# Attention decode with a gated FFN on one core: another wait of the last query, an output product on four quadrants, and a meeting of the engines under the store

## The chip, the cores and the metric

The kernel runs on one core of a Trainium2 chip. The core has five engines with their own instruction streams: TensorE (PE, matrix products; its weight loads are listed as PEld), VectorE (DVE), ScalarE (ACT), GpSimd (POOL) and SyncE (SP, which here issues the transfers). Sixteen DMA engines move data between the chip's main memory and the core's on-chip memory, whose 128 partitions the engines read in parallel. PE writes its sums to a second on-chip memory, PSUM. Engines wait for one another by semaphores.

The metric is the device time of one execution in microseconds, the median of several runs. A profile comes from one further execution.

## The reference

One token goes through a block of attention with a cached K and V, and a gated FFN. Both have a residual and a layer norm in front. All data is float32.

```python
B, Sq, D = 1, 1, 640
H, Sk, Dh = 32, 8192, 192          # 32 heads, 8192 cached positions
F = 1536

q = (x @ wq).reshape(B, Sq, H, Dh)
scores = einsum("bhqd,bhkd->bhqk", q, k_cache) * (Dh ** -0.5)
p = softmax(scores)
o = einsum("bhqk,bhkd->bhqd", p, v_cache)
A(x) = o.reshape(B, Sq, H * Dh) @ wo

gate = x @ W_gate ; up = x @ W_up
B(x) = (gate * (gate > 0) * up) @ W_down

h  = x + A(layernorm(x))
h2 = h + B(layernorm(h))           # the output, 640 numbers
```

K and V of one head take 6.3 MB each, so the execution reads 446 MB in all and computes little with each number.

## The kernel before, in words

Each head's data is packed on the host into two transfers. The first is K (tile `kt`, 12,288 columns on 128 partitions). The second is V together with the head's 192 rows of `wo` and the next head's columns of `wq` (tile `vt0` for heads 1, 3, 5 and so on, `vt1` for heads 2, 4, 6 and so on). There is one `kt` and there are two `vt`. SP issues all loads in one queue, in the order K, V, K, V. It waits for `sp` (the scores of the head before are done, so `kt` is free) ahead of a K, and for `wo` (the output product that reads the same `vt` is done) ahead of a V.

A loop over pairs of heads runs on PE, DVE and ACT. For head n:

- PE makes the scores: 24 products in groups of four quadrants, that is four products of 32 output rows each that use different quarters of the array and of PSUM's partitions (`scores`, tile `sp`).
- PE then finishes the head before: `output(n, vt)` sums the value products over partitions (`po`), DVE's `combine` divides by the softmax's sum and places the head's 192 numbers as two columns in `o` (128 and 64 of them), and PE multiplies them by the rows of `wo` and adds to `acc`, which stays in PSUM for the whole execution. The 64 numbers are first spread by ACT into `o2` (`second`), with zeros in the other half of the partitions, since the 64 rows of `wo` are packed as two halves of 320 columns. PE's last product signals `wo`.
- DVE takes the maximum of the scores on each partition, PE transposes it, DVE takes the maximum of all, ACT makes the exponentials `p` and their sums, PE adds those over partitions (`pl`).
- PE then makes the query of the next head from the `wq` columns in the same `vt` (`query`, five products into `pq`).
- DVE makes 12 value products, j = 0 to 11, each over 1024 columns of `vt` with `p`, with the sum of each partition in `op[:, j]`. Between j = 5 and j = 6 it reads the next query out of `pq` (`columns`), which ACT turns into the operands of the next scores (`masks`).

The last head differs. Its V carries no `wq` columns and comes in four parts (`v0`, semaphores `vb`, `vb1`, `vb2`, `vb3`, three value products each, the fourth with the `wo` rows). DVE waits for each part where it needs it. The loop still makes a next query after it, from old data in the tile, and nobody uses it. For the heads before, the semaphores `vb1` to `vb3` are raised at the start so far that their waits are met.

After the loop come the last output product, ACT's copy of `acc` to `h4` with its sum, the mean and a transpose on DVE, and the FFN. PE multiplies by W_up and W_gate (10 steps of four quadrants), DVE makes the gated product and a transpose, PE multiplies by W_down (12 steps j of four quadrants), DVE adds the residual, and SP stores 640 numbers. The FFN's weights come last in SP's queue: W_up and four fifths of W_gate into `vt0`, the rest of W_gate and W_down (in five transfers) into `kt`. They are issued once the output product of the last but one head is done.

`acc` holds one row of the output, copied over partitions: before, partitions 0 to 63 hold columns 0 to 319, and partitions 64 to 127 the others.

At the end of the program the engines meet at a barrier, POOL clears all semaphores, and they meet again.

Of the kernel before, what the change touches and what calls it, by code (L numbers as in the profile page):

```python
# [6 lines left out]
AF = mybir.ActivationFunctionType  # L7
# [3 lines left out]
P, Q, NQ = 128, 32, 4  # L11
H, S, DH, D, F = 32, 8192, 192, 640, 1536
# [8 lines left out]
D2 = DH - P  # L21
DG, FG, HN = D // NQ, F // NQ, D // 2
KW = S + S // 2
WO = D + HN
# [31 lines left out]
        self.eng.wait_ge(self.c.sem, self.c.n)  # L56


def mha_decode_reglu_kernel(nc, x, w0, kk, vv, v0, w_up, w_gate, w_down, out):
    names = ("w0", "xr", "k", "k2", "va", "vb", "vb1", "vb2", "vb3", "qd", "qs", "sp", "mp", "pt", "m1", "rs",  # L60
             "pl", "q", "op", "po", "o", "o2", "wo", "cst", "st", "ffn0", "ffn1", "ffn2", "ffn3", "ffn4",
             "ffn5", "ffn6", "ffn7", "h4", "hm", "hc", "hr", "pu", "us", "pg", "gu", "pd", "o4", "out")
    s = {n: nc.alloc_semaphore("e_" + n) for n in names}

    def sb(name, shape):
        return nc.alloc_sbuf_tensor(name, shape, F32).ap()

    def ps(name, shape):
        return nc.alloc_psum_tensor(name, shape, F32).ap()
# [4 lines left out]
    xrow = sb("xrow", [1, D])  # L74
    ones = sb("ones", [P, P])
# [5 lines left out]
    blk = sb("blk", [P, NG])  # L81
    blk2 = sb("blk2", [P, NJ - NG])
    half = sb("half", [P, 2])
    side = sb("side", [P, 2, D2])
    pick = sb("pick", [P, 3, 2, C])
    st = sb("st", [P, 16])
    xc = sb("xc", [P, DJ])
# [8 lines left out]
    p = sb("p", [P, SG])  # L96
# [1 line left out]
    rl = sb("rl", [P, 1])  # L98
    op = sb("op", [P, NJ])
    o = sb("o", [P, 2])  # L100
    o2 = sb("o2", [P, P])
    h4 = sb("h4", [P, DG])
    hs1 = sb("hs1", [P, 1])
    hT = sb("hT", [P, DJ, Q])
    hc = sb("hc", [P, DJ, Q])
    hsq = sb("hsq", [P, DJ])
    us = sb("us", [P, FG])
    gu = sb("gu", [P, FG])
    guT = sb("guT", [P, FJ, Q])
    o4 = sb("o4", [P, DG])  # L110
# [6 lines left out]
    acc = ps("acc", [P, QB])  # L117
# [20 lines left out]
    def sync_fn(sy):  # L138
        sy.dma_start(wq0, w0).then_inc(s["w0"], 16)  # L139
        sy.sem_inc(s["k2"], 16 * (H - 1))  # L140
        for n in ("vb1", "vb2", "vb3"):
            sy.sem_inc(s[n], 16 * (H // 2 - 1))
        for h in range(H):
            if h > 0:
                sy.wait_ge(s["sp"], h)
            if h < H - 1:
                sy.dma_start(kt, kk[h]).then_inc(s["k"], 16)
            else:
                sy.dma_start(kt[:, 0:KW // 2], kk[h][:, 0:KW // 2]).then_inc(s["k"], 16)
                sy.dma_start(kt[:, KW // 2:KW], kk[h][:, KW // 2:KW]).then_inc(s["k2"], 16)  # L150
            if h > 0:
                sy.wait_ge(s["wo"], h)
            if h < H - 1:
                sy.dma_start(vts[h % 2], vv[h]).then_inc(s["vb" if h % 2 else "va"], 16)
            else:
                W = JV * SG
                for i, n in enumerate(("vb", "vb1", "vb2", "vb3")):
                    c0, c1 = i * W, (i + 1) * W if i < 3 else KW + WO
                    sy.dma_start(vts[1][:, c0:c1], v0[:, c0:c1]).then_inc(s[n], 16)  # L159
        sy.wait_ge(s["wo"], H)  # L160
        for i, (dst, src, n) in enumerate(ffn):
            if i == 2:
                sy.wait_ge(s["sp"], H)
            sy.dma_start(dst, src).then_inc(s[n], 16)
        sy.wait_ge(s["o4"], 1)
        sy.dma_start(out[0].rearrange("o (g n) -> (o g) n", g=NQ), o4[0:P:Q, :]).then_inc(s["out"], 16)
        sy.wait_ge(s["out"], 16)

    def pool_fn(g):
        c = Chain(nc, g, "e_pool")  # L170
# [16 lines left out]
    def vector_fn(v):  # L187
        c = Chain(nc, v, "e_dve")
        ve, y, t = st[:, 0:1], st[:, 1:2], st[:, 2:3]
# [18 lines left out]
        c.sync()  # L208
        c(v.tensor_copy(same[:, 1:NG, :], same[:, 0:1, :].to_broadcast([P, NG - 1, C])))
        c(v.reduce_sum(blk2, low.rearrange("p (a c) -> p a c", c=C), axis=AX.X))  # L210
        c(v.tensor_copy(side, half[:, :, None].to_broadcast([P, 2, D2])))
        c(v.tensor_copy(pick[:, 2], half[:, :, None].to_broadcast([P, 2, C])))
        c.sync()
        v.sem_inc(s["op"], 1)
# [46 lines left out]
        with v.Fori(1, H + 1, 2) as i:  # L261
            i8 = i * 8 + 8
# [4 lines left out]
        hmean, hs2, hvar, hr = (st[:, i:i + 1] for i in range(9, 13))  # L267
# [20 lines left out]
    def scalar_fn(a):  # L288
        a.dma_start(xrow, x[0]).then_inc(s["xr"], 16)
        sd = st[:, 3:4]  # L290
        a.wait_ge(s["st"], 5)
        a.activation(sd, st[:, 7:8], AF.Sqrt, bias=eps).then_inc(s["st"])
        a.activation(st[0:1, 14:15], eps[0:1, :], AF.Exp)

        def masks(n):
            a.wait_ge(s["qd"], n)
            pk = pick.rearrange("p i a c -> p i (a c)")
            a.mul(qs[:, 0:2, :], pk[:, 0:2, :], q[:, 0:1])  # L298
            a.mul(qs[:, 2, :], pk[:, 2, :], q[:, 1:2]).then_inc(s["qs"])  # L299

        def second(n):
            a.wait_ge(s["o"], n)
            a.mul(o2, side.rearrange("p a c -> p (a c)"), o[:, 1:2]).then_inc(s["o2"])  # L303

        def head(n):
            second(n)
            a.wait_ge(s["m1"], n)
            a.activation(p, sp, AF.Exp, bias=m1, accum_out=rs).then_inc(s["rs"])  # L308
            masks(n + 1)

        masks(1)
        with a.Fori(1, H + 1, 2) as i:
            head(i)
            head(i + 1)
        second(H + 1)
        a.activation(st[0:1, 14:15], eps[0:1, :], AF.Sqrt)
        a.wait_ge(s["wo"], H + 1)
        for g in range(NQ):
            r = slice(g * Q, (g + 1) * Q)
            ins = a.activation(h4[r], acc[r, (g % 2) * DG:(g % 2 + 1) * DG], AF.Copy, accum_out=hs1[r])  # L320
        ins.then_inc(s["h4"])
        a.wait_ge(s["st"], 10)
        a.activation(sd, st[:, 11:12], AF.Sqrt, bias=eps).then_inc(s["st"])
        a.wait_ge(s["hr"], 1)
        a.wait_ge(s["pu"], 1)
        a.activation(us, sp[:, 0:FG], AF.Copy, scale=st[:, 12:13]).then_inc(s["us"])

    def tensor_fn(t):
        def mm(dst, lhsT, rhs, start, stop, **kw):
            return t.matmul(dst, lhsT, rhs, start=start, stop=stop, **kw)  # L330
# [7 lines left out]
        def scores():  # L338
            for u in range(NU):
                if u:  # L340
                    yield
                for k in range(3):
                    for g in range(NQ):
                        c0 = u * (KW // 2) + (k * NQ + g) * QB
                        ins = mm(sp[g * Q:(g + 1) * Q, u * QB:(u + 1) * QB], qs[:, k, :], kt[:, c0:c0 + QB],
                                 k == 0, k == 2)
            ins.then_inc(s["sp"])
            yield

        def output(n, vt):  # L350
            t.wait_ge(s["op"], n)
            mm(po[:, 0:NJ], same.rearrange("p a c -> p (a c)"), op, True, True).then_inc(s["po"])
            t.wait_ge(s["o"], n)
            for i in range(2):
                mm(acc[i * D2:(i + 1) * D2, 0:HN], o[:, 0:1].to_broadcast([P, D2]),
                   vt[:, KW + i * HN:KW + (i + 1) * HN], False, False, skip_group_check=True)
            t.wait_ge(s["o2"], n)
            mm(acc[:, 0:HN], o2, vt[:, KW + D:KW + WO], False, False, skip_group_check=True).then_inc(s["wo"])

        def head(i, b, i8):  # L360
            n = i + b if b else i
            t.wait_ge(s["qs"], n)
            sc = scores()
            k_wait(i, b, "k")
            next(sc)
            k_wait(i, b, "k2")
            next(sc)
            output(n, vts[1 - b])
            t.wait_ge(s["mp"], n)
            t.transpose(pt[:, 0:P], mp.to_broadcast([P, P]), ident).then_inc(s["pt"])  # L370
            t.wait_ge(s["rs"], n)
            mm(pl[:, 0:1], share, rs, True, True).then_inc(s["pl"])
            t.wait_ge(s["vb3" if b else "va"], i8)
            if b:
                t.wait_ge(s["vb"], i8)
            query(vts[b][:, KW + WO:VW])

        def k_wait(i, b, name):
            t.wait_ge(s[name], i * 16 + 16 * b if b else i * 16)
# [2 lines left out]
        t.wait_ge(s["st"], 1)  # L382
        mm(pt[:, 0:1], ones, st[:, 4:5], True, True).then_inc(s["st"])
        t.wait_ge(s["xr"], 16)
        for i in range(2):
            mm(acc[i * D2:(i + 1) * D2, 0:HN], ones[0:1, 0:D2], xrow[:, i * HN:(i + 1) * HN], True, False,
               skip_group_check=True)
        t.wait_ge(s["st"], 3)
        mm(pl[:, 0:1], ones, st[:, 6:7], True, True).then_inc(s["st"])
# [2 lines left out]
        with t.Fori(1, H + 1, 2) as i:  # L392
            i8 = i * 8 + 8
# [25 lines left out]
        for j in range(FJ):  # L419
            if j in cuts:  # L420
                t.wait_ge(s[f"ffn{3 + cuts.index(j)}"], 16)
            for g in range(NQ):
                ins = mm(pq[g * Q:(g + 1) * Q, 0:DG], guT[:, j, :], dn[:, j, g * DG:(g + 1) * DG],
                         j == 0, j == FJ - 1)
        ins.then_inc(s["pd"])

    with nc.Block() as block:
        block.sync(sync_fn)
        block.scalar(scalar_fn)
        block.gpsimd(pool_fn)  # L430
        block.vector(vector_fn)
        block.tensor(tensor_fn)
# [50 lines left out]
```

## Time and profile before

| | us |
|---|---|
| median of 3 runs | 1044.72 |
| lowest, highest | 1044.05, 1044.84 |
| the profiled execution's own time | 1045.74 |
| its span, from first to last instruction | 1043.8 |

| engine | busy us | share of the span |
|---|---|---|
| PE | 453.8 | 43% |
| PEld | 209.0 | 20% |
| DVE | 525.5 | 50% |
| ACT | 77.6 | 7% |
| POOL | 2.1 | 0% |

The profile lists, for each group of like instructions, the line, the engine, the operation, the tiles written and read, their shapes, the number of instructions, the busy time, the mean of one, and the idle time of the engine just before them with what ended it. The chain of waits starts at the last instruction and follows back what released each step. A window can be cut out of each view. PE's clock is not constant: the profile gives the share of full speed that was granted. On average it was 0.657 in this execution.

Nearly all of a float32 matmul's records come as two passes, so that three matmuls stand as x6.

### The profile page before, as it was taken

What the parts mean: (1) busy time and instruction counts of PE and PEld (TensorE: products, weight loads), DVE (VectorE), ACT (ScalarE), POOL (GpSimd) and SP (SyncE); (2) the same over time, 40 slices, a digit from 0 to 9 for tenths busy, and PEclk for the clock granted to TensorE, in tenths of its full rate; (3) what the DMA queues carried; (4) which work ended last, traced back from release to release, by engine and by line L of the source; (5) the groups of instructions that cost most, each with busy time, mean ns of one, the idle gap of its engine ahead of it and who ended that gap; (6) DMA issues with size and microseconds to landing.
All of it is one profiled execution on the core that took longest, in us unless ns stands there. A gap on an engine that the chain in (4) does not pass through costs nothing.

```text
span 1043.8 us, 6624 instructions
## 1 busy us (share of the span) xinstructions
PE 453.8 (43%) x2414; PEld 209.0 (20%) x2414; DVE 525.5 (50%) x1162; ACT 77.6 (7%) x179; POOL 2.1 (0%) x15
## 2 busy tenths in 40 slices
PE   4344353355353355343355343255343255343536
PEld 2122121122121122121122121122121122121213
DVE  1644465644465644465644465644465644465651
ACT  1000000000000000000000000000000000000001
POOL 0000000000000000000000000000000000000000
PEclk9667765666765666676666676766666766665667
DMA  9999999999999999999999999999999999999995
GB/s 397 445 423 429 433 448 422 444 423 431 431 448 422 444 423 429 431 448 424 444 421 431 431 446 424 441 426 431 431 443 426 441 426 431 431 443 426 421 429 247
DMA packets 11102, 445.97 MB, mean 427 GB/s; under 512 B 1237, under 2 KB 1241, under 8 KB 2010
## 3 DMA queue, kind: packets, MB, share of 16 engines
q1 hardware_dynamic: 11096, 445.92, 99.0%
q8 instruction: 2, 0.03, 0.0%
q10 hardware_dynamic: 2, 0.00, 0.0%
q14 instruction: 2, 0.02, 0.0%
HBM read 445.91 MB, written 0.00 MB: 427 GB/s over the span
## 4 chain that ended last, share of the span: by engine, by line
DMA 73%; PE 25%; DVE 1%; issue 0%; ACT 0%; SPq 0%; DVEq 0%
DMA kt<-in_kk_dram 70%; PE sp L330 23%; DMA vt<-in_v_dram 4%; PE pq L330 1%; DVE vt L135 1%; PE acc L330 0%; ACT h L320 0%; SPq L159 0%; DVE junk L135 0%; PE po L330 0%; DVE guT L284 0%; PE pt L330 0%; DVE gu L283 0%; PE pl L330 0%; SPq L139 0%
## 5 line engine op out<-in xcount | busy, mean ns | idle before, releaser
L135 DVE CUSTOM_DVE_ANT_0 vt<-vt,p 128x1024 f32<-128x1024 f32 x384 | 444.9, 1221 | 142.1 <-DMA vt<-in_vv_dram 142.1
L330 PE MATMUL sp<-kt,qs 128*32 128x512 f32 x1536 | 239.7, 789 | 342.1 <-DMA kt<-in_kk_dram 337.6
L330 PE MATMUL pq<-vt,xn 128*128 128x192 f32 x320 | 113.1, 539 | 159.0 <-DMA vt<-in_vv_dram 150.5
L330 PEld LDWEIGHTS sp<-kt,qs 128*32 128x32 f32 x1536 | 55.8, 140 | 512.6 <-DMA kt<-in_kk_dram 359.4
L135 DVE CUSTOM_DVE_ANT_0 junk<-blk,po,rl 128x8 f32<-128x8 f32 x66 | 12.0, 218 | 265.2 <-PE po L330 265.2
L330 PEld LDWEIGHTS pq<-vt,xn 128*128 128x128 f32 x320 | 97.9, 331 | 161.3 <-DMA vt<-in_vv_dram 78.8
L330 PE MATMUL acc<-vt,o 128*64 128x320 f32 (+1 forms) x198 | 50.5, 476 | 15.3 <-DVE o L135 15.3
L303 ACT ACTIVATE o<-side,o 128x128 f32<-128x128 f32 x33 | 13.2, 401 | 478.9 <-DVE o L135 478.9
L298 ACT ACTIVATE qs<-pick,q 128x64 f32<-128x64 f32 x33 | 11.5, 348 | 410.4 <-DVE q L135 410.4
L308 ACT ACTIVATE p<-sp,m 128x1024 f32<-128x1024 f32 x32 | 35.7, 1114 | 50.8 <-DVE m L246 50.8
L244 DVE TENSOR_REDUCE mp<-sp 128x1 f32<-128x1024 f32 x32 | 39.1, 1221 | 0.0
L330 PE MATMUL pl<-rs,share 128*128 128x1 f32 x64 | 16.0, 319 | 51.9 <-ACT p L308 51.9
L248 DVE RECIPROCAL rl<-pl 128x1 f32<-128x1 f32 x32 | 5.4, 169 | 58.5 <-PE pl L330 58.5
L135 DVE DVE_READ_ACCUMULATOR2_ANT op<- 128x1 f32 x384 | 31.9, 83 | 0.0
L330 PEld LDWEIGHTS pl<-rs,share 128*128 128x128 f32 x64 | 13.3, 258 | 62.6 <-ACT p L308 62.6
L330 PEld LDWEIGHTS acc<-vt,o 128*64 128x64 f32 (+1 forms) x198 | 16.6, 154 | 35.1 <-DVE o L135 18.4
L246 DVE TENSOR_REDUCE m<-pt 128x1 f32<-128x128 f32 x32 | 9.3, 292 | 17.9 <-PE pt L370 17.9
L330 PEld LDWEIGHTS po<-op,same 128*128 128x128 f32 x66 | 10.0, 191 | 34.7 <-issue 26.8
L330 PE MATMUL po<-op,same 128*128 128x12 f32 x66 | 13.1, 273 | 7.4 <-DVE op L135 7.4
L135 DVE CUSTOM_DVE_ANT_0 junk<-ident,pq 128x128 f32<-128x128 f32 x33 | 9.3, 283 | 8.7 <-PE pq L330 8.7
L299 ACT ACTIVATE qs<-pick,q 128x32 f32<-128x32 f32 x33 | 10.1, 307 | 0.0
L330 PE MATMUL sp<-vt,hc 128*32 128x384 f32 x72 | 9.1, 669 | 0.6 <-DVE hc L272 0.6
(74 smaller groups left out, 78.4 us busy)
## 6 DMA issues: line engine op xcount, KB each, us to landing
vt<-in_vv_dram SPq DMA_DIRECT2D x31, 7104.0 KB, 38.3
kt<-in_kk_dram SPq DMA_DIRECT2D x31, 6144.0 KB, 23.7
kt<-in_kk_dram SPq DMA_DIRECT2D x2, 3072.0 KB, 20.4
vt<-in_v_dram SPq DMA_DIRECT2D x3, 1536.0 KB, 29.0
vt<-in_w_up_dram SPq DMA_DIRECT2D x1, 3840.0 KB, 19.9
vt<-in_w_gate_dram SPq DMA_DIRECT2D x1, 3072.0 KB, 26.8
vt<-in_v_dram SPq DMA_DIRECT2D x1, 2016.0 KB, 36.6
kt<-in_w_down_dram SPq DMA_DIRECT2D x1, 1920.0 KB, 32.4
```

The source lines that it names most:

```text
L135: return eng.tensor_tensor_reduce(out=res, in0=a, in1=b, scale=scale, scalar=0.0, op0=ALU.mult, op1=ALU.add, accum_out=dst)
L244: v.reduce_max(mp, sp, axis=AX.X).then_inc(s["mp"])
L246: v.reduce_max(m1, pt[:, 0:P], axis=AX.X, negate=True).then_inc(s["m1"])
L248: v.reciprocal(rl, pl[:, 0:1])
L298: a.mul(qs[:, 0:2, :], pk[:, 0:2, :], q[:, 0:1])
L299: a.mul(qs[:, 2, :], pk[:, 2, :], q[:, 1:2]).then_inc(s["qs"])
L303: a.mul(o2, side.rearrange("p a c -> p (a c)"), o[:, 1:2]).then_inc(s["o2"])
L308: a.activation(p, sp, AF.Exp, bias=m1, accum_out=rs).then_inc(s["rs"])
L330: return t.matmul(dst, lhsT, rhs, start=start, stop=stop, **kw)
```

## The change

There are three edits.

First, PE's query in the second head of a pair waits for `vb` alone, where it waited for `vb3` and `vb`.

On PE this is the second head of the loop's pair, from the sum of the value products to the next query. `e_op`, `e_o`, `e_o2`, `e_mp`, `e_rs`, `e_vb` and `e_vb3` are semaphores; `po`, `acc`, `pt`, `pl` and `pq` are tiles in PSUM. Before:

```order
L330 MATMUL po<-op,same 128x12 [waits e_op]
L330 MATMUL acc<-vt,o 64x320 [waits e_o]
L330 MATMUL acc<-vt,o 64x320
L330 MATMUL acc<-vt,o 128x320 [waits e_o2]
L370 MATMUL pt<-ident,mp 128x128 [waits e_mp]
L330 MATMUL pl<-rs,share 128x1 [waits e_rs]
L330 MATMUL pq<-vt,xn 128x192 [waits e_vb,e_vb3]
L330 MATMUL pq<-vt,xn 128x192 x4
```

The same place on PE now:

```order
L326 MATMUL po<-op,same 128x12 [waits e_op]
L326 MATMUL acc<-vt,o 32x160 [waits e_o]
L326 MATMUL acc<-vt,o 32x160 x3
L326 MATMUL acc<-vt,o 32x160 [waits e_o2]
L326 MATMUL acc<-vt,o 32x160 x3
L370 MATMUL pt<-ident,mp 128x128 [waits e_mp]
L326 MATMUL pl<-rs,share 128x1 [waits e_rs]
L326 MATMUL pq<-vt,xn 128x192 [waits e_vb]
L326 MATMUL pq<-vt,xn 128x192 x4
```

The query lost one of its waits, and the three products into `acc` became eight.

Second, the output product goes by quadrants of 160 columns: four products of 32 x 160 with `o`, then four with `o2`, each group on its own quarter of the partitions. `acc` now holds columns 160 g to 160 g + 159 on partitions 32 g to 32 g + 31, all in its first 160 columns. So `side` and `o2` have 64 columns in place of 128, the product that puts x into `acc` at the start has four parts in place of two, and ACT copies `acc` to `h4` by one activation on 128 partitions where it needed four on 32.

On ACT, from the loop's end to its last instruction, before:

```order
L303 ACTIVATE o<-side,o 128x128 [waits e_o]
L316 ACT_TABLE_LOAD
L316 ACTIVATE st<-eps 1x1
L320 ACTIVATE h,hs<-acc 32x160 [waits e_wo]
L320 ACTIVATE h,hs<-acc 32x160 x3
L323 ACTIVATE st<-st,eps 128x1 [waits e_st]
L326 ACTIVATE us<-sp,st 128x384 [waits e_pu,e_hr]
```

The same on ACT now:

```order
L302 ACTIVATE o<-side,o 128x64 [waits e_o]
L315 ACT_TABLE_LOAD
L315 ACTIVATE st<-eps 1x1
L317 ACTIVATE h,hs<-acc 128x160 [waits e_wo]
L319 ACTIVATE st<-st,eps 128x1 [waits e_st]
L322 ACTIVATE us<-sp,st 128x384 [waits e_pu,e_hr]
```

The order stays; the first operation is half as wide, and the four copies are one.

Third, the semaphore of the final store is made outside the block that clears semaphores at its end. SP issues the store and goes to the meeting of the engines; after the clearing and the second meeting it waits for the store and clears that one semaphore.

On SP, the program's end before:

```order
L164 DMA kt<-in_w_down_dram 128x3840
L164 DMA kt<-in_w_down_dram 128x1920
L164 DMA kt<-in_w_down_dram 128x640 x3
L166 DMA out_dram<-o 4x160 [waits e_o4]
L427 UNCONDITIONAL_BRANCH [waits e_out]
```

The same on SP now:

```order
L164 DMA kt<-in_w_down_dram 128x3840
L164 DMA kt<-in_w_down_dram 128x1920
L164 DMA kt<-in_w_down_dram 128x640 x3
L166 DMA out_dram<-o 4x160 [waits e_o4]
L425 UNCONDITIONAL_BRANCH
L481 ISA [waits barrier_Pool_Activation_PE_DVE_SP_release,e_out]
```

The wait for `e_out` moved from ahead of the branch to behind the last barrier, onto the instruction that clears it.

The diff, cut to what matters:

```diff
-def mha_decode_reglu_kernel(nc, x, w0, kk, vv, v0, w_up, w_gate, w_down, out):
+def mha_decode_reglu_kernel(nc, stored, x, w0, kk, vv, v0, w_up, w_gate, w_down, out):
...
-    side = sb("side", [P, 2, D2])
+    side = sb("side", [P, 2, Q])
...
-    o2 = sb("o2", [P, P])
+    o2 = sb("o2", [P, 2, Q])
...
         sy.wait_ge(s["o4"], 1)
-        sy.dma_start(out[0].rearrange("o (g n) -> (o g) n", g=NQ), o4[0:P:Q, :]).then_inc(s["out"], 16)
-        sy.wait_ge(s["out"], 16)
+        sy.dma_start(out[0].rearrange("o (g n) -> (o g) n", g=NQ), o4[0:P:Q, :]).then_inc(stored, 16)
...
-        c(v.tensor_copy(side, half[:, :, None].to_broadcast([P, 2, D2])))
+        c(v.tensor_copy(side, half[:, :, None].to_broadcast([P, 2, Q])))
...
         def second(n):
             a.wait_ge(s["o"], n)
-            a.mul(o2, side.rearrange("p a c -> p (a c)"), o[:, 1:2]).then_inc(s["o2"])
+            a.mul(o2, side, o[:, 1:2]).then_inc(s["o2"])
...
         a.wait_ge(s["wo"], H + 1)
-        for g in range(NQ):
-            r = slice(g * Q, (g + 1) * Q)
-            ins = a.activation(h4[r], acc[r, (g % 2) * DG:(g % 2 + 1) * DG], AF.Copy, accum_out=hs1[r])
-        ins.then_inc(s["h4"])
+        a.activation(h4, acc[:, 0:DG], AF.Copy, accum_out=hs1).then_inc(s["h4"])
...
             t.wait_ge(s["o"], n)
-            for i in range(2):
-                mm(acc[i * D2:(i + 1) * D2, 0:HN], o[:, 0:1].to_broadcast([P, D2]),
-                   vt[:, KW + i * HN:KW + (i + 1) * HN], False, False, skip_group_check=True)
+            for g in range(NQ):
+                mm(acc[g * Q:(g + 1) * Q, 0:DG], o[:, 0:1].to_broadcast([P, Q]),
+                   vt[:, KW + g * DG:KW + (g + 1) * DG], False, False, skip_group_check=True)
             t.wait_ge(s["o2"], n)
-            mm(acc[:, 0:HN], o2, vt[:, KW + D:KW + WO], False, False, skip_group_check=True).then_inc(s["wo"])
+            for g in range(NQ):
+                c0 = KW + D + (g % 2) * DG
+                ins = mm(acc[g * Q:(g + 1) * Q, 0:DG], o2[:, g // 2, :], vt[:, c0:c0 + DG], False, False,
+                         skip_group_check=True)
+            ins.then_inc(s["wo"])
...
-            t.wait_ge(s["vb3" if b else "va"], i8)
-            if b:
-                t.wait_ge(s["vb"], i8)
+            t.wait_ge(s["vb" if b else "va"], i8)
             query(vts[b][:, KW + WO:VW])
...
-        for i in range(2):
-            mm(acc[i * D2:(i + 1) * D2, 0:HN], ones[0:1, 0:D2], xrow[:, i * HN:(i + 1) * HN], True, False,
+        for g in range(NQ):
+            mm(acc[g * Q:(g + 1) * Q, 0:DG], ones[0:1, 0:Q], xrow[:, g * DG:(g + 1) * DG], True, False,
                skip_group_check=True)
...
+    stored = nc.alloc_semaphore("e_out")
     with nc.cleanup_on_exit():
-        mha_decode_reglu_kernel(nc, *args)
+        mha_decode_reglu_kernel(nc, stored, *args)
+    nc.sync.wait_ge(stored, 16)
+    nc.sync.sem_clear(stored)
```

More of the change, by code (lines that the diff above doesn't have):

```diff
@@ L56, in sync @@
         self.eng.wait_ge(self.c.sem, self.c.n)
-def mha_decode_reglu_kernel(nc, x, w0, kk, vv, v0, w_up, w_gate, w_down, out):
+def mha_decode_reglu_kernel(nc, stored, x, w0, kk, vv, v0, w_up, w_gate, w_down, out):
     names = ("w0", "xr", "k", "k2", "va", "vb", "vb1", "vb2", "vb3", "qd", "qs", "sp", "mp", "pt", "m1", "rs",
              "pl", "q", "op", "po", "o", "o2", "wo", "cst", "st", "ffn0", "ffn1", "ffn2", "ffn3", "ffn4",
-             "ffn5", "ffn6", "ffn7", "h4", "hm", "hc", "hr", "pu", "us", "pg", "gu", "pd", "o4", "out")
+             "ffn5", "ffn6", "ffn7", "h4", "hm", "hc", "hr", "pu", "us", "pg", "gu", "pd", "o4")
     s = {n: nc.alloc_semaphore("e_" + n) for n in names}
```

## The prediction

> **What bounds the kernel now.** I read the page's head, its queue table and its groups first. In the group row, the two numbers behind the bar are the busy time and the mean of one instruction in ns; behind the second bar stands the idle time ahead of them and what ended it.
>
> ```profile
> span 1043.8 us, 6624 instructions
> ...
> q1 hardware_dynamic: 11096, 445.92, 99.0%
> ...
> L135 DVE CUSTOM_DVE_ANT_0 vt<-vt,p 128x1024 f32<-128x1024 f32 x384 | 444.9, 1221 | 142.1 <-DMA vt<-in_vv_dram 142.1
> ```
>
> The loads keep the 16 DMA engines busy for 99.0% of the span, and DVE waits for V in all 31 heads that are loaded whole: 142.1 / 31 = 4.6 us each. So inside the loop the transfers set the pace, and a shorter PE step there only lengthens a wait. What the change can win lies after the last V. There I read the chain of waits (start, us, what):
>
> ```profile
> 970.74 36.56 DMA vt<-in_v_dram
> ...
> 1007.34 3.58 PE pq L330 x10
> ...
> 1010.94 0.29 DVE junk L135
> ...
> 1017.11 1.14 DVE vt L135
> ...
> 1018.31 0.61 PE po L330 x2
> ...
> 1019.38 2.71 PE acc L330 x6
> ...
> 1022.11 0.39 ACT h L320 x2
> ...
> 1023.85 0.21 ACT h L320
> ...
> 1025.28 1.51 PE sp L330 x8
> ...
> 1027.30 8.23 PE sp L330 x72
> ...
> 1035.63 0.57 DVE gu L283
> ...
> 1036.23 0.85 DVE guT L284
> ...
> 1037.12 3.51 PE pq L330 x96
> ...
> 1040.66 0.38 DVE o L286
> ```
>
> The reader sees the last part of the last V land at 1007.30, then an unused query (3.58 us), then six value products of DVE (1010.94 to 1018.27), the output product, the copy of the sum by ACT, the up and gate projections (1025.28 to 1035.53), the down projection (1037.12 to 1040.63) and the store. No transfer stands in the chain after 1007.30. But the FFN's weights are still coming at that time, and the question is how much of the chain can move forward before it runs into them. The timeline gives the issue of each load, the page the time from issue to landing, and the last row, for tile kt's loads from 996 us on, the longest of them:
>
> ```profile
> 996.52 0.33 SPq L164 DMA_DIRECT2D vt<-in_w_up_dram  x1
> 996.89 0.43 SPq L164 DMA_DIRECT2D vt<-in_w_gate_dram  x1
> 997.84 3.38 SPq L164 DMA_DIRECT2D kt<-in_w_down_dram  x5
> ```
>
> ```profile
> vt<-in_w_up_dram SPq DMA_DIRECT2D x1, 3840.0 KB, 19.9
> vt<-in_w_gate_dram SPq DMA_DIRECT2D x1, 3072.0 KB, 26.8
> ...
> kt<-in_w_down_dram SPq DMA_DIRECT2D x1, 1920.0 KB, 32.4
> ```
>
> ```profile
> L164 SPq DMA_DIRECT2D kt<-in_w_down_dram x5: 334/426/1213, 997.8 to 1000.0; - x5
> ...
> DMA to landing us min/median/max: 28.2/34.1/35.0
> ```
>
> W_up has landed at 996.5 + 19.9 = 1016.4, four fifths of W_gate at 996.9 + 26.8 = 1023.7, the first half of W_down (its six first j) at 997.8 + 32.4 = 1030.2, and the last twelfth of W_down at 1000.0 + 35.0 = 1035.0. The remaining fifth of W_gate stands in the queue between the second and the third of these, 768 of 2688 KB on, so by my estimate at 1025.6.
>
> **The query's wait.** PE now waits for the first part of the last V only. In the last head it is free after the sum of the softmax, and DVE has done its first six products at 1005.87:
>
> ```profile
> 998.23 0.59 PE L330 MATMUL pl<-rs,share 128*128 128x1 f32 x2 [1.62 <-ACT p L308]
> ...
> 1005.79 0.08 DVE L135 DVE_READ_ACCUMULATOR2_ANT op<- 128x1 f32 x1
> ```
>
> The query runs 998.8 to 1002.4 (3.58 us, the cold price above) and lies wholly beside DVE's products. DVE reads its result at 1005.9 in place of 1010.94: 5.04 us earlier. The products of j = 9 to 11 need the last part, landed at 1007.30; three products of 1.14 us put j = 9 at 1009.8, so no new wait comes there. Nothing is queued behind this wait on PE but the output product, which needs DVE anyway. In all other heads the removed wait was already met (the counter starts 240 high), so it costs and gives nothing there.
>
> **The output product.** Two matmuls of 64 x 320 and one of 128 x 320 become four and four of 32 x 160; PE records each as two passes. Passes follow one another except that four quadrants run together: before, 4 sequential passes of 320 columns took 2.71 us at the tail's clock; afterwards 4 sequential groups of 160 columns are half of the streaming. From the row of the same form (the down projection, 96 passes in 3.51 us, 0.146 us a group of four at full clock, 0.29 at half), 4 groups take 1.2 us, plus one start of some 0.3 us (two passes of a single column, pl above, took 0.59). The bounds are 1.2 us and, if only loading and issuing counted and nothing were saved, 2.71; I take 1.5, nearest to the row of the same form. But ACT takes over. After o is known at 1019.33 it makes o2, loads a table and takes a root:
>
> ```profile
> 1019.36 0.40 ACT L303 ACTIVATE o<-side,o 128x128 f32<-128x128 f32 x1 [7.38 <-DVE o L135]
> ...
> 1019.77 1.28 ACT L316 ACT_TABLE_LOAD   x1
> ...
> 1021.07 0.20 ACT L316 ACTIVATE st<-eps 1x1 f32<-1x1 f32 x1
> ```
>
> ```profile
> L298 ACT ACTIVATE qs<-pick,q 128x64 f32<-128x64 f32 x33 | 11.5, 348 | 410.4 <-DVE q L135 410.4
> ```
>
> A 128x64 multiplication took 348 ns where o2 takes 0.40 us today, so ACT is free 1.89 us after o in place of 1.94, and copies acc then, not 2.78 us after o: a gain of 0.89. In the 32 heads of the loop the shorter product frees V's buffer and lets the transpose go some 0.5 us earlier; the 4.6 us of waiting for V take that up, so zero.
>
> **The copy of the sum.** Four activations with their reads of the accumulator ran from 1022.11 to 1024.06, 1.95 us. One over 128 partitions has the same 160 columns for each lane: 1.95 / 4, about 0.50. Gain 1.45; bounds 0 (were the time to grow with the partitions) and 1.46.
>
> **Where the gain stops.** The three make 5.04 + 0.89 + 1.45 = 7.38 us. The up projection would start at 1017.9, after its weights (1016.4). It needs 7.1 us at half clock, from 1025.28 to 1032.4:
>
> ```profile
> 1032.40 0.58 ACT L326 ACTIVATE us<-sp,st 128x384 f32<-128x384 f32 x1 [4.57 <-PE sp L330]
> ```
>
> So it ends at 1025.0, after W_gate's 1023.7, and the gate at 1028.2. The down projection would then be ready at 1029.7, before its weights: 1030.2 for half of them, 1035.0 for the last. What is late next is the end of the loads. PE does six j in 6 x 0.29 = 1.75 us, the others as they land, and ends one j after the last, at 1035.0 + 0.3 = 1035.34 in place of 1040.63. Of 7.38 us, 5.29 remain.
>
> **The end.** SP's own rows of before, a wait and a step:
>
> ```profile
> 1041.07 0.65 SPq L166 DMA_DIRECT2D out_dram<-o  x1
> ```
>
> ```profile
> SPq L427 <- DMA out_dram<-o: 1.0, 1, 1.0
> ```
>
> ```profile
> L479 POOLq EVENT_SEMAPHORE_RANGE_CLEAR  x1: 287/287/287, 1043.3 to 1043.3; - x1
> ```
>
> SP issued until 1041.72 and waited to about 1042.76; meeting, clearing and meeting again took the remaining 1.04 us to the span's end at 1043.8. Done under the store, these end when the store does; SP then clears one semaphore. That price is not shown: below 0.29 (POOL clears the whole range in that), above zero. I take the dearer, since it is the row of the same operation: gain 1.04 - 0.29 = 0.75.
>
> The smaller `side` and the four short matmuls of the start lie 1000 us ahead of the end, beside the first loads: nothing.
>
> **Sum.** 5.29 + 0.75 = 6.04 us. The profiled execution took 1045.74, that is 1.94 around its span, and would take 1039.70. It stands 1.02 above the median of the runs shown, 1044.72; applied to that: 1038.7.
>
> **Rivals.** *PE goes cold in the waits.* Down's j come with gaps, and a cold PE needs twice the 3.51 us. The clock by stage (the column after POOL's is the granted clock):
>
> ```profile
> 1014.73:1018.14 3.41, 0.00 (x0) 0.00 (x0) 3.41 (x7) 0.00 (x0) 0.00 (x0) 0.50 1.01 434
> ...
> 1028.40:1031.80 3.40, 3.40 (x28) 1.07 (x24) 0.29 (x2) 0.00 (x0) 0.00 (x0) 0.50 0.97 397
> 1031.80:1035.50 3.70, 3.68 (x48) 1.19 (x40) 0.00 (x0) 0.58 (x1) 0.00 (x0) 1.00 0.44 165
> 1035.50:1037.10 1.60, 0.00 (x0) 0.00 (x0) 1.40 (x2) 0.00 (x0) 0.00 (x0) 1.00 0.00 0
> 1037.10:1040.70 3.60, 3.47 (x96) 3.02 (x96) 0.04 (x1) 0.00 (x0) 0.00 (x0) 1.00 0.00 0
> ```
>
> It rose only at 1031.8, 6.5 us into the projections, and stayed over a gap of 1.6 us. Now the gap is 2.0 us (1028.2 to 1030.2), or more where the clock rises sooner and the gate ends with its weights. All twelve j cold from 1030.2 are 7.0 us: PE ends at 1037.2, 1.85 later, 1040.5 in all. For it: the idle stretch at half clock. Against: the gap that kept it, and that a late drop costs one or two j of 0.3 us.
> The Trainium skill (TensorE: Matmul & The Clock Gate, Part 1) has the clock rise after one busy window of about 3.4 us, free-running, and fall after an idle one. By that rule the projections may warm as early as 3.4 us after their start, leaving a gap long enough to lose the clock again; the trace's one rise came at 6.5 us, which the free-running window allows.
>
> *The clock does not rise at all.* Then up and gate, whose j cost (7.1 - 1.51 - 0.5) / 4 = 1.27 us cold, take 7.1 + 6.4 = 13.5 in place of 10.25, down starts at 1033.0 and ends at 1040.0: a gain of 0.6 + 0.75, 1043.4, no change to speak of. Against: the 1.00 after 6.5 us of the same work.
>
> *SP's step before the meeting waits for its store.* Then the end does not do what it says; the one more clear costs up to 0.29: 5.29 - 0.29 = 5.0, 1039.7. No row shows SP passing that step with a transfer open.
>
> *Slower: every pass pays its own start.* If quadrants did not overlap at all, each of the 16 passes would cost 0.295 us of start (pl's 0.59 for two) and 0.29 of cold streaming, 9.4 us a head against 2.71, a growth of 6.7. It decides from 4.6 us of growth on, DVE's spare in a head: (6.7 - 4.6) x 31 = 65 us more, 1110. Against: 96 passes of this very form in 3.51 us, 0.037 each.
>
> **Chances.** My forecast 0.66, its own range 1037.8 to 1039.6 (the end's bounds, and 0.4 us to each side as the runs spread); a cold down projection 0.12; SP's store waited for 0.12; a gain beyond mine 0.02; no rise of the clock 0.05; a start for every pass 0.03. A change under 0.2%, 2.1 us, can't be told from none here. So faster 0.92, same 0.05, slower 0.03. The range reaches up to both smaller gains together, 1044.72 - (5.29 - 1.85 - 0.29) = 1041.6, and down to 1037.7.
>
> **What would show it.** Profile after: PE's last query ends by 1003 and DVE's products run on without the gap that lay between 1005.87 and 1010.94; the copy of acc starts right behind ACT's root and takes 0.5; PE's down projection waits for W_down and ends some 0.3 after its last landing; SP's last wait is for the store, after the clear. I am wrong if the loads end at another time than 1035, if the down projection runs at half clock, or if the wait at DVE's sixth product stays.

## The result and the profile after

| | before | after |
|---|---|---|
| median, us | 1044.28 (5 runs) | 1039.56 (5 runs) |
| lowest to highest, us | 1044.05 to 1044.84 | 1039.51 to 1039.79 |
| profiled execution, us | 1045.74 | 1039.79 |
| span of the profiled execution, us | 1043.8 | 1038.0 |

The changed kernel is faster by 4.72 us in the median. The ratio is 0.9954, with a 95% interval of 0.994 to 0.9969. Between the two profiled executions the difference is 5.95 us.

The page of the changed kernel, in the same rows as before:

```profile
span 1038.0 us, 7270 instructions
...
q1 hardware_dynamic: 11096, 445.92, 99.5%
...
L135 DVE CUSTOM_DVE_ANT_0 vt<-vt,p 128x1024 f32<-128x1024 f32 x384 | 445.0, 1222 | 146.6 <-DMA vt<-in_vv_dram 146.6
```

The same bytes came in a span that is 5.8 us shorter. In the loop DVE waits for V a little longer than before, 146.6 / 31 = 4.7 us a head instead of 4.6. The shorter output product lets the transpose come sooner: DVE's waits for it fell from 17.3 to 12.9 us over the loop. These 4.4 us became waiting for V, which grew by 4.5.

The chain of waits of the changed kernel, its last links (start, us, what):

```profile
996.67 0.90 PE acc L326 x16
...
1001.10 33.86 DMA kt<-in_w_down_dram
1034.96 0.04 issue
1035.00 0.52 PE pq L326 x8
1035.53 0.02 issue
1035.55 0.39 DVE o L285
```

The chain no longer passes through the query, the value products and the projections. It goes from the issue of W_down's last transfer at 1001.10 to its landing at 1034.96, and only the last j of the down projection and the residual stand behind that. The timeline shows how PE got there:

```profile
1000.21 3.55 PE L326 MATMUL pq<-vt,xn 128*128 128x192 f32 x10
...
1007.33 0.28 DVE L135 CUSTOM_DVE_ANT_0 junk<-ident,pq 128x128 f32<-128x128 f32 x1
...
1014.55 0.08 DVE L135 DVE_READ_ACCUMULATOR2_ANT op<- 128x1 f32 x1
...
1015.74 0.35 ACT L302 ACTIVATE o<-side,o 128x64 f32<-128x64 f32 x1 [7.38 <-DVE o L135]
...
1015.76 1.29 PE L326 MATMUL acc<-vt,o 128*32 128x160 f32 x16 [0.47 <-DVE o L135]
...
1017.40 0.20 ACT L315 ACTIVATE st<-eps 1x1 f32<-1x1 f32 x1
1017.51 0.28 ACT L317 ACTIVATE h<-acc 128x160 f32<-128x160 f32 x1
1017.69 0.19 ACT L317 ACTIVATION_READ_ACCUMULATOR h<-acc 128x1 f32 x1
...
1030.39 1.84 PE L326 MATMUL pq<-kt,guT 128*32 128x160 f32 x48 [2.61 <-DMA kt<-in_w_down_dram]
```

The unused query lies beside DVE's products, DVE has no gap at its sixth product, and the copy of the sum is one instruction pair that starts right behind ACT's root. PE stands idle for 2.61 us ahead of the down projection. The gated product and its transpose fill this time up to 1029.37; the last 1.0 us is a wait for the first half of W_down. The clock stayed up meanwhile (the columns after the stretch: its length, the busy time and count of PE, PEld, DVE, ACT and POOL, the granted clock, the DMA share, GB/s):

```profile
1019.10:1022.55 3.45, 3.44 (x22) 1.30 (x26) 1.31 (x8) 0.29 (x1) 0.00 (x0) 0.50 0.88 374
1022.55:1027.80 5.25, 5.23 (x67) 1.69 (x56) 0.01 (x1) 0.58 (x1) 0.00 (x0) 1.00 1.03 429
1027.80:1030.30 2.50, 0.00 (x0) 0.00 (x0) 1.40 (x2) 0.00 (x0) 0.00 (x0) 1.00 0.96 401
1030.30:1035.60 5.30, 4.09 (x96) 2.70 (x96) 0.05 (x1) 0.00 (x0) 0.00 (x0) 1.00 0.55 211
```

At the end of the program SP no longer waits between store and meeting. Its steps before the meeting, of before and of after:

```profile
L427 SPq COMPARE_BRANCH  x1: 38/38/38, 1042.8 to 1042.8; - x1
L427 SPq DRAIN  x1: 7/7/7, 1042.9 to 1042.9; - x1
```

```profile
L425 SPq DRAIN  x1: 417/417/417, 1036.7 to 1036.7; - x1
```

```profile
L481 SPq EVENT_SEMAPHORE_RANGE_CLEAR  x1: 25/25/25, 1038.0 to 1038.0; - x1
```

With the store open SP's drain took 417 ns where it took 7 ns before. The clear of the one semaphore took 25 ns.

### The profile page after: what moved, and what is told of

It reads as the page before. It is cut to its first block, busy times and chain, and to the rows that moved or that the text cites. A ratio compares the mean times of both kernels' runs of the same rounds, so it can differ in the third digit from the quotient of the medians.

```text
span 1038.0 us, 7270 instructions
## 1 busy us (share of the span) xinstructions
PE 440.6 (42%) x2748; PEld 203.7 (20%) x2748; DVE 525.4 (51%) x1162; ACT 74.3 (7%) x173; POOL 2.1 (0%) x15
## 4 chain that ended last, share of the span: by engine, by line
DMA 76%; PE 23%; SPq 0%; issue 0%; DVE 0%
DMA kt<-in_kk_dram 73%; PE sp L326 23%; DMA kt<-in_w_down_dram 3%; SPq L164 0%; PE acc L326 0%; PE pq L326 0%; SPq L139 0%; DVE o L285 0%; DVE junk L135 0%; PE po L326 0%; SPq L149 0%; SPq L142 0%; DVE o L135 0%; SPq L140 0%
## 5 line engine op out<-in xcount | busy, mean ns | idle before, releaser
L135 DVE CUSTOM_DVE_ANT_0 vt<-vt,p 128x1024 f32<-128x1024 f32 x384 | 445.0, 1222 | 146.6 <-DMA vt<-in_vv_dram 146.6
L302 ACT ACTIVATE o<-side,o 128x64 f32<-128x64 f32 x33 | 11.5, 348 | 480.0 <-DVE o L135 480.0
L326 PE MATMUL acc<-vt,o 128*32 128x160 f32 x528 | 28.8, 316 | 15.3 <-DVE o L135 15.3
L326 PEld LDWEIGHTS acc<-vt,o 128*32 128x32 f32 x528 | 10.6, 109 | 25.8 <-DVE o L135 18.4
L370 PE MATMUL pt<-ident,mp 128*128 128x128 f32 x32 | 10.3, 323 | 8.9 <-DVE mp L243 8.9
```

Source lines behind the costliest of these rows:

```text
L135: return eng.tensor_tensor_reduce(out=res, in0=a, in1=b, scale=scale, scalar=0.0, op0=ALU.mult, op1=ALU.add, accum_out=dst)
L302: a.mul(o2, side, o[:, 1:2]).then_inc(s["o2"])
```

## The experiments

Two questions were open. Does the end now come from the loads (theory L), or do the parts simply add up (rival S)? And why is the gain 4.7 us in the median, when it is 5.95 between the profiles and 6.04 was forecast? For the second, theory C says that the kernel before depends on the moment at which PE's clock rises, and that its profiled execution had a late one; rival P says that the profile itself lengthened that execution. Each comparison is with runs of the kernel before on the same chip, whose median was 1044.93 (19 runs), 1044.6 (27) and 1044.53 (21) in the three groups below.

### One part alone, and one part undone

The query's wait alone:

```diff
-            t.wait_ge(s["vb3" if b else "va"], i8)
-            if b:
-                t.wait_ge(s["vb"], i8)
+            t.wait_ge(s["vb" if b else "va"], i8)
```

> The kernel before with the query's wait changed alone. Theory L (the changed kernel ends when its loads end): DVE's products end 5 us sooner, the down projection meets its last weights at 1035, PE ends at 1035.5 and the span at about 1038.3 to 1038.7; against a usual PE end of 1039.2 in the kernel before this is a gain of 3.7 us, about 1040.6. Rival S (the gains of the parts add up, none runs into the loads): the query gives what is left of 4.72 once the other two parts have given theirs of 2.3 and 0.7, so 1.7 us, about 1042.6.

Measured: 1040.76 us (1040.35 to 1041.33), ratio 0.9956 (0.9943 to 0.997), a gain of 4.17. Its chain ends as that of the changed kernel:

```profile
999.93 35.17 DMA kt<-in_w_down_dram
...
1035.15 0.52 PE pq L330 x8
```

The old output product and the old copy do not keep this kernel from its loads. L's 1040.6 holds, S's 1042.6 does not.

The output product on quadrants alone, with the old wait of the query and the old end (the diff is against the changed kernel):

```diff
...
-        sy.dma_start(out[0].rearrange("o (g n) -> (o g) n", g=NQ), o4[0:P:Q, :]).then_inc(stored, 16)
+        sy.dma_start(out[0].rearrange("o (g n) -> (o g) n", g=NQ), o4[0:P:Q, :]).then_inc(s["out"], 16)
+        sy.wait_ge(s["out"], 16)
...
-            t.wait_ge(s["vb" if b else "va"], i8)
+            t.wait_ge(s["vb3" if b else "va"], i8)
+            if b:
+                t.wait_ge(s["vb"], i8)
...
-    stored = nc.alloc_semaphore("e_out")
     with nc.cleanup_on_exit():
-        mha_decode_reglu_kernel(nc, stored, *args)
-    nc.sync.wait_ge(stored, 16)
-    nc.sync.sem_clear(stored)
+        mha_decode_reglu_kernel(nc, *args)
...
```

> The kernel before with the output product on quadrants alone. Both theories: the chain behind the last product is 2.3 us shorter (0.9 at the product, 1.45 at the copy of the sum) and the loads, which end at 1035.0, are still covered, so about 1042.0, and the time still varies from run to run with the moment at which PE's clock rises. If the loop counted the product, 31 heads of 0.6 us would give some 19 us more.

Measured: 1042.24 us (1041.29 to 1043.06), ratio 0.9972 (0.9962 to 0.9981), a gain of 2.7 where 2.3 was expected. The chain behind the last value product got shorter: in the profile, from that product's end to the start of the projections, it took 1022.61 - 1018.15 = 4.46 us, and 1025.28 - 1018.27 = 7.01 before. The product of 31 heads, which would have been worth some 19 us if the loop counted it, gave nothing that shows beside this.

The meeting under the store alone:

```diff
-        sy.dma_start(out[0].rearrange("o (g n) -> (o g) n", g=NQ), o4[0:P:Q, :]).then_inc(s["out"], 16)
-        sy.wait_ge(s["out"], 16)
+        sy.dma_start(out[0].rearrange("o (g n) -> (o g) n", g=NQ), o4[0:P:Q, :]).then_inc(stored, 16)
...
+    nc.sync.wait_ge(stored, 16)
+    nc.sync.sem_clear(stored)
```

> The kernel before with the meeting under the store alone. Both theories: 0.7 us less, about 1043.6; SP's last step before the meeting takes some tenths of a us with the store open where it took 7 ns without. If that step waited for the store, 0.

Measured: 1044.31 us (1043.33 to 1044.76), ratio 0.9992 (0.9983 to 1.0001), 0.62 less in the median with an interval that just reaches no change. So the times alone do not show this gain. The profiles are sharper: from the store's issue to the end of the span it is 1043.8 - 1041.07 = 2.73 us before and 1038.0 - 1035.96 = 2.04 us in the changed kernel, whose store was issued at 1035.96:

```profile
1035.96 0.65 SPq L166 DMA_DIRECT2D out_dram<-o  x1
```

In the profile of this run the store was issued at 1040.08 and the span ended at 1042.1, so 2.0 us again, and SP's drain took 418 ns.

The changed kernel with the old wait of the query:

```diff
-            t.wait_ge(s["vb" if b else "va"], i8)
+            t.wait_ge(s["vb3" if b else "va"], i8)
+            if b:
+                t.wait_ge(s["vb"], i8)
```

> The changed kernel with the old wait of the query. Theory L: 2.3 + 0.7 us of gain, about 1041.3; the chain sets the end, and the spread from run to run is back. Theory S: the gain less 1.7, about the same 1041.3; this run and the query alone together tell the theories apart (L: the two gains, 3.7 and 3.0, exceed the whole 4.72 by 2 us; S: they sum to it).

Measured: 1040.78 us (1040.77 to 1041.78), ratio 0.9961 (0.9947 to 0.9974), a gain of 4.15 where 3.0 was expected; the parts alone gave 2.7 + 0.6 = 3.3. Its profiled execution ends by the chain of work, as expected: 6.88 us of projections behind the first group, then the gated product, the transpose and 3.51 us of down projection, with no landing between.

```profile
1024.54 6.88 PE sp L326 x72
...
1031.52 0.57 DVE gu L282
...
1033.01 3.51 PE pq L326 x96
```

The query alone gives 4.17 and the rest alone 4.15. They sum to 8.3, where the whole gives 4.7 to 4.9. So the parts overlap, as L has it, by more than the 2 us expected. Part of what this run gained beyond the expected 3.0 lies in the clock. The next profile of the kernel before, shown further down, had its last value product end at the same 1018.06. Beside it the profile of this run is 2.57 us shorter ahead of the projections, 0.5 in them, where they took 8.9 us in place of 9.4, and 0.7 at the end.

The changed kernel with the old output product and copy, that is the query's wait and the meeting:

```diff
...
-        sy.dma_start(out[0].rearrange("o (g n) -> (o g) n", g=NQ), o4[0:P:Q, :]).then_inc(s["out"], 16)
-        sy.wait_ge(s["out"], 16)
+        sy.dma_start(out[0].rearrange("o (g n) -> (o g) n", g=NQ), o4[0:P:Q, :]).then_inc(stored, 16)
...
-            t.wait_ge(s["vb3" if b else "va"], i8)
-            if b:
-                t.wait_ge(s["vb"], i8)
+            t.wait_ge(s["vb" if b else "va"], i8)
...
+    stored = nc.alloc_semaphore("e_out")
     with nc.cleanup_on_exit():
-        mha_decode_reglu_kernel(nc, *args)
+        mha_decode_reglu_kernel(nc, stored, *args)
+    nc.sync.wait_ge(stored, 16)
+    nc.sync.sem_clear(stored)
...
```

(This diff is against the kernel before.)

> The changed kernel with the old output product and copy (query's wait and meeting changed). Theory L: the 2.3 us that the quadrants save in the chain lie beside the loads, so within 0.4 us of the changed kernel, about 1039.6 to 1040.0. Theory S: 2.3 us slower than the changed kernel, about 1041.9.

Measured: 1039.86 us (1039.73 to 1040.22), ratio 0.9956 (0.9942 to 0.997). That is 0.3 us from the changed kernel's 1039.56, where the same edit alone was worth 2.7. Its chain of waits ends as work, with no transfer in it:

```profile
1031.91 3.55 PE pq L329 x96
1035.46 0.02 issue
1035.48 0.38 DVE o L285
```

PE started down at 1031.91 and went through without a wait of its own; only one weight load waited 0.2 us for W_down. It was done at 1035.46, practically where the changed kernel's PE is done (1035.52). So here the work and the loads end together. In the changed kernel, whose down projection could have started at 1029.4, the quadrants add some 2.5 us of slack, and next to no time.

### More to load

1.57 MB more, columns of K that nobody reads, put into a free part of `kt` ahead of the rest of W_gate and of W_down. The first kernel is the changed one, the second the one before:

```diff
+XC = F + FJ * D
...
             if i == 2:
                 sy.wait_ge(s["sp"], H)
+                sy.dma_start(kt[:, XC:KW], kk[0][:, XC:KW]).then_inc(s["more"], 16)
             sy.dma_start(dst, src).then_inc(s[n], 16)
+        sy.wait_ge(s["more"], 16)
         sy.wait_ge(s["o4"], 1)
```

> The changed kernel with 1.57 MB more to load (columns of K that nobody reads, into a free part of kt, ahead of W_down). At 430 GB/s that is 3.65 us. Theory L: the end moves by all of it, about 1043.2. If the chain of work set the end, W_down would only have to come before PE reaches it and the end would move by less than 1.5 us.

> The kernel before with the same 1.57 MB more to load. Its PE reached the last weights 5 us after their landing in the profile, some 4 us in a usual execution, so the 3.65 us lie under the chain of work: 0 to 0.4 us more, about 1044.4. If the loads set its end, 3.65 us more, 1047.9.

Measured: the changed kernel went to 1043.44 us (1043.17 to 1044.39), the kernel before to 1045.13 (1044.13 to 1046.04; ratio 1.0005, 0.9996 to 1.0014). Against the changed kernel's 1039.56 that is 3.9 us more (3.65 were expected), against 1044.6 it is 0.5. So the same transfer costs all of its time in the one kernel and next to nothing in the other. That is the clearest sign that the change has moved the end from the chain of work to the loads. In the first of them PE's clock also fell. PE had waited 2.73 us for the last part of W_gate and worked on it for 0.85; the clock fell at 1029.96, as this work ended, and stayed down over the wait for W_down:

```profile
1023.14:1029.96 6.82, 4.09 (x48) 1.09 (x40) 0.00 (x0) 0.58 (x1) 0.00 (x0) 1.00 1.02 431
1029.96:1033.80 3.84, 0.02 (x3) 0.01 (x1) 1.40 (x2) 0.00 (x0) 0.00 (x0) 0.50 0.96 405
1033.80:1036.79 2.99, 2.96 (x48) 2.52 (x52) 0.00 (x0) 0.00 (x0) 0.00 (x0) 0.50 0.92 355
1036.79:1039.00 2.21, 2.13 (x56) 1.47 (x48) 0.01 (x1) 0.00 (x0) 0.00 (x0) 1.00 0.13 47
```

```profile
1033.83 5.14 PE pq L329 x96
1038.97 0.02 issue
```

The first 3 us of the down projection ran at half clock, and PE was still done 0.57 us after the last landing (1038.4), against 0.56 in the changed kernel: while it was slow, the later parts of W_down were still on their way.

### PE kept busy

Products of 128 x 192 that nobody reads, 11 ahead of the last output product and 3 behind it in the kernel before, and 14 and 1 in the changed one:

```diff
+    dm = ps("dm", [P, QB])
...
+        def busy(n):
+            for _ in range(n):
+                mm(dm[:, 0:DH], ones, wq0[:, 0:DH], True, True)
...
+        busy(11)
         output(H + 1, vts[1])
+        busy(3)
```

> The kernel before with 14 products that nobody reads put on PE where it is idle between the last query and the FFN (11 ahead of the last output product, 3 behind it), so that its clock is up. Theory C (the moment at which the clock rises sets the kernel before's end and its spread): output product and projections run at full clock, 3 to 4 us less than the profile's 1045.7 to 1045.0 and about 1041 in the median, with a spread below 0.4 us. Rival P (the profile itself made the profiled execution of before 1 us longer): the median moves by no more than 1 us.

> The changed kernel with 15 products that nobody reads put on PE where it idles between the last query and the FFN, so that its clock is up. Theory L: the projections are done sooner and the down projection waits longer for its weights, so no change within 0.3 us, 1039.4 to 1039.8. If the chain of work set the end, 1 us or more less.

Measured: the kernel before went to 1042.2 us (1041.31 to 1045.61), ratio 0.9982 (0.9973 to 0.9991); the changed one stayed, 1039.6 (1039.48 to 1039.69). In the profiled execution of the first, which was the fastest of its eleven, the whole of the projections ran at full clock and took 1031.22 - 1024.07 = 7.15 us in place of 10.25:

```profile
1019.98:1023.40 3.42, 3.31 (x10) 2.46 (x8) 0.46 (x1) 2.77 (x10) 0.00 (x0) 0.50 0.94 393
1023.40:1031.30 7.90, 7.19 (x83) 2.69 (x82) 1.80 (x10) 0.88 (x2) 0.00 (x0) 1.00 0.98 407
```

So the clock does set the kernel before's end. But the expectation of a median near 1041 and of a spread below 0.4 us failed: the clock still fell for one stretch in that profile (1019.98 to 1023.40), and the times spread over 4.3 us. The spread lies inside the span, which ran from 1039.5 to 1043.8 us, but only the fastest execution has a profile, and what slowed the others stays open. In the changed kernel the same products gave nothing. There the clock fell at 1030.90, 0.64 us into the down projection, behind an idle PE of 3.14 us, and the down projection ran most of its time at half clock:

```profile
1030.90:1034.31 3.41, 3.41 (x60) 3.41 (x56) 0.00 (x0) 0.00 (x0) 0.00 (x0) 0.50 0.68 257
```

```profile
1030.26 5.17 PE pq L327 x96
1035.43 0.03 issue
```

PE was done at 1035.43 all the same.

### Both kernels unchanged, for more profiles

> The kernel before, unchanged, for another profile and more times. Theory C: its span differs from the first profile's 1043.8 by as much as the time from the start of the up projection to the end of the gate differs from 10.25 us, its loads still end at 1035.0, and the times spread over 1.5 us. Rival P: the profiled execution again lies 1 us above the median, with the projections at 10.25 us.

> The kernel before once more, as the run before: a third profile to set the span beside the duration of the projections and the moment at which the clock rises. Theory C: 2 us of span between an early rise (3.4 us into the projections) and a late one (6.8 us).

> The changed kernel, unchanged, for another profile. Theory C and L: whatever the clock does in its projections, the down projection waits for its last weights, the span is 1037.8 to 1038.1 and the times spread by less than 0.4 us.

Measured: the kernel before gave 1044.71 us (1044.05 to 1046.0; ratio to itself 1.0004, 0.9995 to 1.0013) and 1045.31 (1044.58 to 1046.26; 1.0007, 0.9997 to 1.0017), the changed one 1039.65 (1039.54 to 1039.87; 0.9957, 0.9943 to 0.997). The projections of the first of these, with the clock about them:

```profile
1025.09 1.51 PE sp L330 x8
1026.59 0.52 PE pl L330 x2
1027.11 7.37 PE sp L330 x72
```

```profile
1025.09:1029.86 4.77, 4.77 (x30) 1.68 (x34) 1.31 (x8) 0.29 (x1) 0.00 (x0) 0.50 0.99 415
1029.86:1034.50 4.64, 4.56 (x56) 1.44 (x48) 0.00 (x0) 0.58 (x1) 0.00 (x0) 1.00 0.68 262
```

Here the clock rose 4.8 us into the projections, and they took 9.4 us; in the first profile it rose after 6.5, and they took 10.25. The difference of 0.86 us is half of the 1.75 us by which the rise came later, as it must be when the clock doubles. The span was 1042.8 in place of 1043.8, with the start of the projections 0.2 earlier. The second of these runs had the rise at 4.9 us, projections of 9.5 and again a span of 1042.8. The loads ended at 1034.8, 1034.6 and, in the first profile, 1035.0. So in these three profiles the span follows the clock's rise, as C has it. The 2 us between an early and a late rise were not seen, since no profile of the kernel before had the early one; by the half just worked out they would be 1.7. The first profile was a long execution: the spans of the 67 executions of the kernel before in the three groups lie between 1042.0 and 1043.6 us, and its own was 1043.8. The changed kernel's profile had a span of 1037.9 and its times spread over 0.33 us, as expected. One thing does not fit: the profiled execution of the second run of the kernel before took 1045.70, 2.9 us around its span, where the others had 1.8 and 1.9. That part of the spread lies outside what the profile shows, and its cause stays open. Rival P fails: the profiled execution of the first of these runs came out at 1044.56, below the median of 1044.71 of its own eleven.

## Why the prediction was right, and where it was off

**Direction and mechanism.** Right. The forecast was that 7.4 us of the chain would go and that the loads would stop the gain at the last landing. The chain of waits after, the transfer added to both kernels, and the edits made alone show this. The time itself was forecast 0.9 us too low: 1039.56 lies only 0.04 inside the upper end of the range, because of the step from profile to median below.

**The loads' end.** Forecast 1035.0, landed at 1034.96.

**The query's wait.** Forecast: DVE reads the query at 1005.9. It did so at 1007.33, since in this execution most of the last head's scores ran at half clock (4.48 us from 991.41, where the profile before had 2.78 us) and all of the head came later. The query ended at 1003.76 and not by 1003 for the same reason. The step's statement holds: DVE went on without a gap and without a new wait at j = 9.

**Output product and copy.** Forecast 1.5 us for the product with ACT taking over 1.89 us after o, and 0.50 for the copy. Measured 1.29, and the copy began 1017.51 - 1015.71 = 1.80 after o and took 0.37. The two gains of 0.89 + 1.45 were in truth 2.6 together. All of it lies beside the loads, as forecast.

**When the down projection is ready.** Forecast 1029.7, measured 1029.4, but by two errors that cancel. The projections started at 1019.11 in place of 1017.9, and took 8.7 us in place of 10.3, since the clock rose 3.4 us after their start and not 6.5. That agreement is luck. No time hung on it, because W_down's first half was awaited either way.

**From the last landing to PE's end.** Forecast 0.3, measured 0.56: the row had the cost of one j in a stream, 0.29, and one j by itself took 0.52. (The recorded 1035.34 also stands 0.04 above the sum of its own rounded terms.) Of the forecast 5.29 us, 1040.63 - 1035.52 = 5.11 came.

**The end.** Forecast 0.75, measured 2.73 - 2.04 = 0.69, by other terms. The clear cost 25 ns and not up to 287. SP's drain, which I had taken as free in the main case and as waiting for the whole store in a rival, took 417 ns with the store open. So that rival was partly right. The two errors, 0.26 in favour and 0.41 against, nearly cancel, which was luck; they leave 0.60, and the other 0.09 of the measured 0.69 was not traced.

**The step from profile to median.** This is the term that was mis-sized. The sum for the profiled execution, 1045.74 - 6.04 = 1039.70, agrees with the 1039.79 of the changed kernel's profiled execution. Of the 5.95 us between the two, 5.11 + 0.69 = 5.80 are span; the other 0.15 is luck in the time around the span, 1.94 us before and 1.79 after. But I then took off the 1.02 us by which the first profile stood above the median, as if the changed kernel would keep the same distance. That 1.02 lay in the stretch that the change takes off the path: beside the next profile of the kernel before, 0.86 us of it can be seen as the clock's late rise in the projections, and 0.2 as their later start. The changed kernel waits there, so the excess vanished with the change and could not be subtracted again. The forecast of 1038.7 is 0.9 below the measured 1039.56, and the gain of 6.04 should have been 5.0 against a median execution.

**The rivals.** The clock fell at or just behind PE's waits in the changed kernel of two experiments (PE busy, more to load), as the rival said, while in the changed kernel itself it stayed up over the idle 2.61 us. The rival's price of 1.85 us was not paid in any of them: it assumed all of W_down to be there at the start of the down projection, and a PE at half clock loses only what the later landings don't hide. The Trainium skill (TensorE: Matmul & The Clock Gate, Part 1) has the clock fall after an idle window of about 3.4 us. The two stretches above agree with it in part: the clock rose again 6.83 and 3.41 us after its fall, two such windows and one, but the idle PE ahead of the falls lasted 2.73 and 3.14 us, each followed by some work, and no whole 3.4 us. No clock that stayed down and no price for each pass was seen: 16 passes took 0.90 us in the loop and 1.29 at the end.

## What to carry to other kernels

When a chain is shortened that runs beside a stream of loads, look up the landing of each load first: it tells how much of the gain can come, and an absolute time for the end is safer than a difference. Take a difference from profile to median only for time that the change leaves on the path; if the profiled execution was late in the very stretch that goes, its excess goes as well. And a wait that is met in all iterations but the last still costs its full time there, when no other work is left to cover it.

## What was unexpected in the hardware

SP's drain took 417 ns with a store of 2.5 KB on its way and 7 ns without, though it didn't wait for the landing: it ended at 1037.1, and the store's packets moved at 1037.2 to 1037.3. The part of a time outside the span was 1.8 us in most profiled executions and 2.4 to 2.9 in three of them (1045.70 - 1042.8 for the kernel before, 1041.33 - 1038.9 with the query alone, 1044.59 - 1042.1 with the meeting alone), and no view of the profile says why. The changed kernel with more to load spread over 1.2 us though it ends at its loads. Its spans spread by as much, from 1041.4 to 1042.6; the cause stays open.
